# A second level of the seven-product scheme in one product of a down projection

## The chip, the cores and the metric

The kernel runs on 1 core of a Trainium2 chip. The metric is the device time in microseconds (us) of one execution; three runs of the kernel before gave 717.07, 717.15 and 718.08 us, a median of 717.15. Engines are named as in the profile: PE is TensorE (matmuls), PEld its weight loads, DVE VectorE, ACT ScalarE, POOL GpSimd, SP SyncE (here only a DMA queue).

## The reference

One transformer-like block over x of 2048 rows by 1024 columns, in bf16:

```python
xn = _layernorm(x, axis=-1)
s = _A_ref(xn, A_wqkv, A_wo)      # attention: 32 heads of 32; each row sees 8 rows, 2 apart, back; softmax; @ wo
g = _silu(_B_ref(xn, B_w1, B_w3, B_w2))
return x + s * g
def _B_ref(x, w1, w3, w2):        # w1, w3: 1024 x 3584; w2: 3584 x 1024
    gate = jnp.einsum("bsd,df->bsf", x, w1)
    up = jnp.einsum("bsd,df->bsf", x, w3)
    h = _silu(gate) * up
    return jnp.einsum("bsf,fd->bsd", h, w2)
```

The change is in the last line of `_B_ref`, the down projection `h @ w2`.

## The kernel before, in words

**Work.** The 2048 rows are worked through as two blocks of 1024 rows (`b` = 0, 1); a block is two chunks of 512 rows ("row" 0 and 1; chunks are counted c = 0 to 3), and a chunk is four groups of 128 rows (`g`). Every block goes through the q, k, v projections, the up projections, the down projection (`mlp_down`) and, chunk by chunk, attention and the output projection `wo`. The attention itself (products, logits, softmax, weighted sums) is DVE work that fills the time beside PE's matmuls of other stages: chunk 0's beside block 0's up projection, chunk 1's beside block 0's down projection and block 1's q, k, v, and so on.

**Seven products instead of eight.** Every large product is already done by the scheme of Strassen and Winograd at one level: operands are cut in halves (rows, inner dimension, columns), DVE forms sums S1 to S4 of the left operand and T1 to T4 of the right one, and seven half-size products replace eight. In `mlp_down` the left operand is h, 1024 rows by 3584 (28 tiles of 128, FH = 14 in a half), the right one w2, 3584 by 1024 (two column halves of CH = 512). S1 to S4 are formed by DVE in the stage itself (lines 1018 to 1023 and 1033); T1 to T4 were formed while block 0's q projection ran and lie in DRAM (`t_dram`). The seven products follow one another on PE, each as 4 groups x 14 matmuls of 512 columns: h00 w00 into banks `pa` (line 1016), h01 w10 (1026), S2 T2 into `pb` (1035), **S1 T1 into `pe` (1040 to 1044)**, then into `pe` again the product with w2's second half (1055, its right operand called V here), S3 T3 and T4's product into `pb` (1060, 1066). ACT and DVE copy and add the banks between (`dsu`, `dsp`, `dsb`, `dsa`).

**S1** lies in `xs` and part of `xT` (block 0: one place per group; block 1: in `xT`, two groups side by side; `s1v`, line 976).

**Buffers.** The right operands are loaded by SP into a ring of six buffers of 8 KB per partition (pool `r8`): every load takes the two next free buffers, 7 tiles (NQ) each. In block 0 the same ring also holds the rows of chunks 2 and 3 (`xn[0]`, `xn[1]`, called x2 and x3 here), which are normalised in the stage and turned into `xT` by transposing DMAs issued by ACT (`ln_turn`, line 520; `turn2_0` to `turn2_3` after the products marked ("pr", 4 + g), chunk 3's after ("pr", 12) and ("pr", 15)).

**What sets the order.** The program lists its operations with what they read and write (`plan.op`, `tt` for a DVE sum, `cp` for an ACT copy, `dma`). `Plan.place` gives each slot of a pool the buffer that was last used longest ago, and everything that uses the new slot waits for everything that used the old one. PE keeps the order of the listing. For the other engines and queues `Plan.limits` works out when each operation is due (back from PE's order), and `Plan.simulate` runs a clock: whenever an engine is free it takes, of the operations that are ready by that clock, the one that is due first. That order is then written into the program and the chip keeps it: an engine does its instructions in the planned order, whatever is ready. `plan.soon` makes named operations due earlier, `plan.rank` puts named ones first, `plan.chains` puts one after another. In that clock all DMAs go through one pipe:

```python
            if o.nbytes:
                pipe = max(pipe, T + occ + 0.9) + o.nbytes / o.rate
                o.done = pipe + 1.3
```

with `o.rate` 3e5 bytes per us in this stage, and `hop` adds 0.1.

Of the kernel before, what the change touches and what calls it, by code (L numbers as in the profile page):

```python
# [209 lines left out]
def kernel(  # L210
# [737 lines left out]
    def mlp_down(b):  # L948
        G = range(NST)
        R = [range(0, FH), range(FH, FT)]  # L950
        F_ = [slice(0, FH), slice(FH, FT)]
        gs = [[slice(rr * CH + g * P, rr * CH + (g + 1) * P) for g in G] for rr in range(2)]

        def rhs_load(kind, fh=0, dh=0, t=0):
            res = []
            for q in range(FH // NQ):
                wt = plan.slot("r8", f"d{kind}")
                dt = FP16 if kind == "t" else BF16
                v = lambda wt=wt, dt=dt: r8v(wt, dt)[:, 0:NQ * CH].rearrange("p (k n) -> p k n", k=NQ)
                if kind == "t":  # L960
                    dma(SP, "t2", v, lambda q=q: t_dram[:, q * NQ:(q + 1) * NQ, t, :],
                        [("td", i) for i in range(q * NQ, (q + 1) * NQ)], [wt], 896)
                else:
                    f = fh * FH + q * NQ
                    dma(SP, "w2", v, lambda f=f: w2_r[:, f:f + NQ, dh * CH:(dh + 1) * CH], [], [wt], 896)
                res.append((wt, [lambda k=k, v=v: v()[:, k, :] for k in range(NQ)]))
            return res

        def prod(ps, g, row, fh, rhs, first, dt, mark=()):
            src = h_sb if dt == BF16 else h16  # L970
            for q, (wt, ops) in enumerate(rhs):
                fs = range(fh * FH + q * NQ, fh * FH + (q + 1) * NQ)
                mm(ps, [lambda f=f: src[:, f, gs[row][g]] for f in fs], ops, first and q == 0,
                   [wt] + h_cells(fs, row, [g]), last=q == 1, mark=mark)

        def s1v(g):

            if b + 1 == NB:
                return xT16[:, g // 2].rearrange("p k n -> p (k n)")[:, 0:FH * 256].rearrange(
                    "p (f n) -> p f n", f=FH)[:, :, (g % 2) * P:(g % 2 + 1) * P]  # L980
            if g < 3:
                return xs[:, g].rearrange("p k n -> p (k n)")[:, 0:FH * P].rearrange("p (f n) -> p f n", f=FH)
            return xT16[:, 1, 0:FH // 2, CH // 2:CH].rearrange("p k (s n) -> p k s n", s=2)

        def s1_k(g, k):
            return s1v(g)[:, k // 2, k % 2, :] if b + 1 < NB and g == 3 else s1v(g)[:, k, :]

        def s1_cells(g):
            if b + 1 == NB:
                return [("xT", g // 2, f, g % 2) for f in range(FH)]  # L990
            return xs_cells(g) if g < 3 else xt_cells(1, 0, 2) + xt_cells(1, 1, 2) + xt_cells(1, 0, 3) + xt_cells(1, 1, 3)

        def fit(g, a):

            return (lambda: a().rearrange("p (k s) n -> p k s n", s=2)) if b + 1 < NB and g == 3 else a

        hb = lambda fh, row, g: (lambda: h_sb[:, F_[fh], gs[row][g]])
        hf = lambda fh, row, g: (lambda: h16[:, F_[fh], gs[row][g]])
        hcl = lambda fh, row, g: h_cells(R[fh], row, [g])
        NS = FH * P  # L1000
        rhs = rhs_load("w", 0, 0)
        xn = []
        for c in range(2 * b + 2, 2 * b + 4 if b + 1 < NB else 0):
            xt = plan.slot("r8", f"x{c}")
            xn.append(xt)
            for st in range(NST):
                x_load(c, st, xt)
            plan.shift = -5.0
            ln_act(c, range(NST), xt)
            plan.shift = 0.0  # L1010
        pa, pb = [], []
        for g in G:
            if g == 2:
                flush()
            pa.append(bank(f"da{b}_{g}"))
            prod(pa[g], g, 0, 0, rhs, True, BF16)
        for g in G:
            tt("s1", add, lambda g=g: s1v(g), fit(g, hb(0, 1, g)), fit(g, hb(1, 1, g)), hcl(0, 1, g) + hcl(1, 1, g), s1_cells(g), NS, True)
            tt("s3", sub, hf(0, 1, g), hb(0, 0, g), hb(0, 1, g), hcl(0, 0, g) + hcl(0, 1, g), hcl(0, 1, g), NS, True)
        for g in G:  # L1020
            pb.append(bank(f"db{b}_{g}"))
            cp("dfork", pb[g].ap, pa[g].ap, [pa[g]], [pb[g]])
            tt("s2", sub, fit(g, hf(0, 0, g)), lambda g=g: s1v(g), fit(g, hb(0, 0, g)), s1_cells(g) + hcl(0, 0, g), hcl(0, 0, g), NS, True)
        rhs = rhs_load("w", 1, 0)
        for g in G:
            prod(pa[g], g, 0, 1, rhs, False, BF16, [("pr", 4 + g)])
            if b + 1 < NB:
                ln_turn(2 * b + 2, g, xn[0], ("pr", 4 + g))
            gsilu(2 * b, 0, g, pa[g].ap, [pa[g]], 0.48)
        rhs = rhs_load("t", t=T2)  # L1030
        su2 = []
        for g in G:
            tt("s4", sub, hf(1, 0, g), hb(1, 0, g), hf(0, 0, g), hcl(1, 0, g) + hcl(0, 0, g), hcl(1, 0, g), NS, True)
        for g in G:
            prod(pb[g], g, 0, 0, rhs, False, FP16, [("pr", 8 + g)])
            su2.append(plan.slot("k2", "dsu"))
            cp("dsu", lambda g=g: f32(su2[g]), pb[g].ap, [pb[g]], [su2[g]])
        rhs = rhs_load("t", t=T1)
        pe, sp5 = [], []
        for g in G:  # L1040
            pe.append(bank(f"de{b}_{g}"))
            for q, (wt, ops) in enumerate(rhs):
                mm(pe[g], [lambda g=g, k=k: s1_k(g, k) for k in range(q * NQ, (q + 1) * NQ)], ops, q == 0,
                   [wt] + s1_cells(g), last=q == 1, mark=[("pr", 12 + g)])
            if b + 1 < NB and g == 0:
                ln_turn(2 * b + 3, 0, xn[1], ("pr", 12))
                ln_turn(2 * b + 3, 1, xn[1], ("pr", 12))
            if b + 1 < NB and g == 3:
                ln_turn(2 * b + 3, 2, xn[1], ("pr", 15))
                ln_turn(2 * b + 3, 3, xn[1], ("pr", 15))  # L1050
            sp5.append(plan.slot("k2", "dsp"))
            cp("dsp", lambda g=g: f32(sp5[g]), pe[g].ap, [pe[g]], [sp5[g]])
        rhs = rhs_load("w", 1, 1)
        for g in G:
            prod(pe[g], g, 0, 1, rhs, False, FP16, [("pr", 16 + g)])
            tt("dsb", add, lambda g=g: f32(su2[g]), pe[g].ap, lambda g=g: f32(su2[g]), [pe[g], su2[g]], [su2[g]], 512, False)
            gsilu(2 * b, 1, g, lambda g=g: f32(su2[g]), [su2[g]], 0.54)
        rhs = rhs_load("t", t=T3)
        for g in G:
            prod(pb[g], g, 1, 0, rhs, False, FP16, [("pr", 20 + g)])  # L1060
            tt("dsa", add, lambda g=g: f32(sp5[g]), pb[g].ap, lambda g=g: f32(sp5[g]), [pb[g], sp5[g]], [sp5[g]], 512, False)
            gsilu(2 * b + 1, 1, g, lambda g=g: f32(sp5[g]), [sp5[g]], 0.54)
        rhs = rhs_load("t", t=T4)

        def t4(g):
            prod(pb[g], g, 1, 1, rhs, False, BF16, [("pr", 24 + g)])
            gsilu(2 * b + 1, 0, g, pb[g].ap, [pb[g]], 0.48)

        def t4_last():

            g = NST - 1
            dst, wr = gate(2 * b + 1, 0, g)
            prod(pb[g], g, 1, 1, rhs, False, BF16)
            for h in range(2):
                silu("dgh", half(dst, h), half(pb[g].ap, h), [pb[g]], wr + [("gate", h)], 0.25)

        last = b + 1 == NB
        for g in G[:-1] if last else G:
            t4(g)
        return t4_last if last else None  # L1080
# [4 lines left out]
    def wo_tc(q):  # L1085
        return h_cells([2 * q, 2 * q + 1], 0) + h_cells([2 * q, 2 * q + 1], 1)

    def wo_load():

        wots = []  # L1090
        for dh in range(2):
            wot = plan.slot("r8", f"wo{dh}")
            dma(SP, "wo", lambda wot=wot: wot.ap().rearrange("p (j n) -> p j n", j=NJ),
                lambda dh=dh: wo_r[:, :, dh * CH:(dh + 1) * CH], [], [wot], 1024)
            wots.append(wot)
        return wots
# [178 lines left out]
    for nm in "qk":  # L1275
        for j in range(4):
            plan.rank[f"fsnap{nm}{j}"] = len(plan.rank)
    plan.chains.append("qs5q0 qs5q1 qforkq0 qforkq1".split())
    for st in range(NST):
        if st == 2:  # L1280
            ln_mix(0, 2, x0)
# [18 lines left out]
    for b in range(NB):  # L1300
# [43 lines left out]

        def first(b=b):
            if b:
                w1o.extend(wo_load())
            else:
                up_load(b, 0)

# [6 lines left out]
            up_step(b, fb)  # L1357
        attention(c0)
        t4_last = mlp_down(b)
        wots = wo_load()  # L1360
        wo_sums(wots)
        wo(c0, wots)
    attention(3)
    wo(3, wots, last=t4_last)
    flush()
    plan.soon = {n + c: -200.0 for c in "03" for n in ("L", "z", "tr", "zd", "exp", "rec", "pb", "E")}
    plan.run()


# [28 lines left out]
```

## Time and profile before

| | us |
|---|---|
| runs: lowest, median, highest | 717.07, 717.15, 718.08 |
| the profiled execution: span from first to last instruction | 715.3 |
| PE busy, DVE busy, ACT busy in that span | 707.4, 643.8, 382.3 |
| block 0's down projection, PE, from and to | 250.6 to 337.0 |
| its S1 T1 product | 288.6 to 300.7 |
| block 1's S1 T1 product | 639.1 to 651.2 |
| the last matmul starts | 711.6 |

The profile holds one execution's span; its time with what lies around it isn't recorded, so the span is set beside the median, 1.85 us above it. Times in the views are counted from the span's start. A timeline row has the start, the length, the engine, the source line, the operation with what it writes and reads (`out<-in`, by the names of pools and tensors: `r` is the r8 ring, `mm` the PSUM banks, `k` the k2 pool, `a` the attention pool), the form and the count; in brackets, how long the engine had been idle before it and what ended that. The line is mostly that of a helper (L322 the matmul of `mm`, L331 the sum of `tt`, L336 the copy of `cp`, L359 `dma`, L523 `ln_turn`), so operations are told apart by tile, form and time. Engines overlap successive instructions a little, so a row's start is a better measure than its length.

### The profile page before, as it was taken

How to read it: one execution, taken by the hardware profiler on the slowest of the kernel's cores; microseconds unless marked ns; L12 is line 12 of the kernel's file. 1: busy time of each engine (PE TensorE's matmuls, PEld its weight loads, DVE VectorE, ACT ScalarE, POOL GpSimd, SP SyncE). 2: the span in 40 equal slices, each digit the busy share in tenths (PEclk: the TensorE clock that was granted, in tenths of full speed). 3: DMA queues.
4: the chain of work that ended last, by engine and by line, in shares of the span. 5: the costliest groups of instructions: out<-in, count | busy, mean ns of one | idle time of the engine just before them, and what ended most of it. 6: DMA issues, size and time to landing. Idle time of an engine off the chain costs nothing.

```text
span 715.3 us, 9199 instructions
## 1 busy us (share of the span) xinstructions
PE 707.4 (99%) x3287; PEld 343.0 (48%) x3342; DVE 643.8 (90%) x866; ACT 382.3 (53%) x650; POOL 50.7 (7%) x103
## 2 busy tenths in 40 slices
PE   9999999999999999999999999999999999999998
PEld 5555544444444444444555554444444444444443
DVE  7999999997999999599999999676999995899936
ACT  7644556575656799142545354676565654411133
POOL 1020100202000000202000000211000002200000
PEclk9999999999999999999999999999999999999999
DMA  9999966659644758994553569787537347655502
GB/s 331 290 358 345 350 224 203 222 155 300 207 148 169 258 181 237 212 269 125 174 170 131 180 198 337 261 283 244 173 129 239 114 153 213 214 191 177 177 21 97
DMA packets 132205, 151.34 MB, mean 212 GB/s; under 512 B 17216, under 2 KB 109248, under 8 KB 127808
## 3 DMA queue, kind: packets, MB, share of 16 engines
q1 hardware_dynamic: 117168, 121.98, 53.4%
q0 software_dynamic: 6112, 26.22, 10.2%
q10 hardware_dynamic: 8880, 2.56, 1.8%
q8 instruction: 26, 0.43, 0.2%
q14 instruction: 19, 0.16, 0.1%
HBM read 106.96 MB, written 32.51 MB: 195 GB/s over the span
## 4 chain that ended last, share of the span: by engine, by line
PE 99%; issue 0%; DVE 0%; ACT 0%; DVEq 0%
PE mm L322 97%; PE mm L307 1%; PE mm L501 0%; DVE xT L331 0%; ACT xT L508 0%; DVE r L435 0%; PE mm L347 0%; DVE k L305 0%; ACT small L424 0%; DVEq L1393 0%; DVE small L426 0%; DVE eps_t L290 0%; DVE eps_d L291 0%; DVEq L331 0%
## 5 line engine op out<-in xcount | busy, mean ns | idle before, releaser
L322 PEld LDWEIGHTS <-r 128*128 128x128 f16 (+1 forms) x2276 | 240.0, 107 | 244.5 <-DMA r<-in_A_wqkv_dram 0.5
L322 PE MATMUL mm<-xs,r 128*128 128x512 f16 x1280 | 295.2, 379 | 0.0
L322 PE MATMUL mm<-xT,r 128*128 128x512 bf16 (+2 forms) x956 | 224.3, 371 | 2.1
L336 ACT COPY k<-mm 128x512 f32<-128x512 f32 x192 | 112.4, 586 | 93.5 <-PE mm L322 93.0
L322 PE MATMUL mm<-r,h_sb 128*128 128x512 bf16 (+1 forms) x694 | 153.0, 379 | 0.5
L322 PEld LDWEIGHTS <-h_sb 128*128 128x128 f16 (+1 forms) x800 | 78.3, 98 | 94.4
L336 ACT COPY mm<-mm 128x512 f32<-128x512 f32 (+1 forms) x89 | 50.6, 571 | 72.2 <-PE mm L322 68.2
L331 DVE TENSOR_TENSOR a<-a,a 128x2048 bf16<-128x2048 bf16 (+1 forms) x72 | 87.7, 1218 | 0.3
L331 DVE TENSOR_TENSOR a<-qo,kT 128x2048 bf16<-128x2048 bf16 x64 | 77.4, 1219 | 1.4 <-ACT kT L336 1.3
L331 DVE TENSOR_TENSOR a<-E,vT 128x2048 bf16<-128x2048 bf16 x56 | 66.4, 1217 | 0.0
L331 DVE TENSOR_TENSOR k<-mm,k 128x512 f32<-128x512 f32 x72 | 48.1, 684 | 19.9 <-PE mm L322 19.8
L331 DVE TENSOR_TENSOR h_sb<-mm,k 128x512 bf16<-128x512 f32 x96 | 63.0, 684 | 1.0 <-PE mm L322 0.5
L353 ACT ACTIVATE k<-k 128x512 bf16<-128x512 f32 x56 | 34.9, 631 | 45.6 <-DVE k L331 45.6
L331 DVE TENSOR_TENSOR h_sb<-h_sb,k 128x1024 bf16<-128x1024 bf16 x56 | 37.1, 686 | 17.2 <-ACT k L336 17.2
L331 DVE TENSOR_TENSOR r<-r,r 128x1024 f16<-128x1024 f16 (+5 forms) x61 | 49.5, 818 | 0.9 <-DMA xT<-r 0.5
L353 ACT ACTIVATE h_sb<-mm 128x512 bf16<-128x512 f32 x60 | 35.8, 598 | 21.7 <-PE mm L322 21.6
L331 DVE TENSOR_TENSOR a<-a 128x1024 bf16<-128x1024 bf16 (+4 forms) x60 | 37.9, 633 | 6.8 <-ACT a L754 4.4
L336 ACT CAST k<-mm 128x512 bf16<-128x512 f32 x56 | 32.6, 585 | 12.2 <-PE mm L322 12.1
L331 DVE TENSOR_TENSOR qo<-qo,a 128x2048 bf16<-128x2048 bf16 x32 | 38.9, 1216 | 0.0
L359 POOL DMA_DIRECT2D a<-E x32 | 16.7, 528 | 303.6 <-ACT k L336 126.1
L331 DVE TENSOR_TENSOR h_sb<-h_sb 128x512 f16<-128x512 bf16 (+1 forms) x72 | 37.0, 575 | 0.0
L331 DVE TENSOR_TENSOR r<-r 128x1024 f16<-128x1024 bf16 (+1 forms) x34 | 25.7, 780 | 0.0
(98 smaller groups left out, 387.8 us busy)
## 6 DMA issues: line engine op xcount, KB each, us to landing
r<-in_B_w_dram SPq DMA_DIRECT2D x42, 512.0 KB, 4.3
s_dram<-r POOLq DMA_DIRECT2D x14, 1024.0 KB, 5.4
r<-t_dram SPq DMA_DIRECT2D x16, 896.0 KB, 6.1
r<-s_dram SPq DMA_DIRECT2D x14, 1024.0 KB, 4.8
r<-in_B_w_dram SPq DMA_DIRECT2D x12, 896.0 KB, 4.9
r<-in_A_wqkv_dram SPq DMA_DIRECT2D x10, 1024.0 KB, 7.3
h_sb<-in_B_w_dram SPq DMA_DIRECT2D x14, 512.0 KB, 8.9
t_dram<-h_sb POOLq DMA_DIRECT2D x14, 512.0 KB, 6.5
```

The lines of the kernel that those rows point to most:

```text
L307: nc.tensor.matmul(plan.pools["mm"][i % 8][:], lhsT=warm[:, 0:P], rhs=warm[:, 0:CH], start=True, stop=True)
L322: nc.tensor.matmul(cut(ps.ap()), lhsT=lhs[k](), rhs=cut(rhs[k]()), start=(first and k == 0), stop=(last and k == n - 1), skip_group_check= ...
L331: plan.op(DVE, name, lambda: fn(out=o(), in0=a(), in1=b()), rd, wr, occ, 0.08, late=late)
L336: plan.op(ACT, name, lambda: nc.scalar.copy(out=o(), in_=a()), rd, wr, occ, 0.11)
L353: plan.op(ACT, name, lambda: nc.scalar.activation(out=o(), in_=a(), func=ACTF.Silu), rd, wr, occ, 0.11, table="silu")
L359: plan.op(eng, name, lambda: e.dma_start(out=o(), in_=a()), rd, wr, occ, 0.0, nbytes=kb * 1024, late=late)
```

## The change

The product S1 T1 (512 x 1792 by 1792 x 512) is itself done by seven products of half the size, in both blocks. Its operands are cut once more: rows in two pairs of groups (`m`), the 14 inner tiles in even and odd ones (`kk`), the columns in two halves of 256 (`n`). Its T1 load therefore takes every second tile (`fs`), and all of T1 is loaded before. `product2` forms the second level's sums on DVE: u (the sum S1 of this level) and t1 in a new r8 slot `ex`, the others in place. Each of the 14 calls of `p` per block is 7 matmuls of 256 columns (`NQ`). The bank of one group is used in halves of 256 columns, with ACT copies (`l2s15`, `l2fork`, `l2u2`) and DVE adds (`l2c22`, `l2c12`) between. S2 T2's product for the last group, `t2(NST - 1)`, moves between the first four and the last ten of these calls, and the four `dsp` copies and chunk 3's turns stand behind all of them. Apart from that: the loads get names, block 0's first `wo` load is chained behind the second half of T4's load on SP, and chunk 1's logit DMAs and softmax steps get the early due times that chunks 0 and 3 had.

```diff
                 if kind == "t":
-                    dma(SP, "t2", v, lambda q=q: t_dram[:, q * NQ:(q + 1) * NQ, t, :],
-                        [("td", i) for i in range(q * NQ, (q + 1) * NQ)], [wt], 896)
+                    fs = slice(q, FH, 2) if t == T1 else slice(q * NQ, (q + 1) * NQ)
+                    dma(SP, f"t2_{b}{t}{q}", v, lambda fs=fs: t_dram[:, fs, t, :],
+                        [("td", i) for i in range(FH)[fs]], [wt, (wt, 0), (wt, 1)], 896)
...
+        def product2(pe, rhs):
+            ex = plan.slot("r8", "ex")
+            HC = CH // 2
...
+            for a, u, cells, uc, size in rows:
+                tt("l2s1", add, u, a(1, 0), a(1, 1), cells(1, 0) + cells(1, 1), uc, size, True)
+            in_place((1, 0), (0, 0), True, "l2s3")
+            tt("l2t1", sub, tv, wv(0, 1), wv(0, 0), [(w[0], 1), (w[0], 0)], [(ex, 0)], NQ * HC, True)
+            tt("l2t3", sub, wv(0, 1), wv(1, 1), wv(0, 1), [(w[1], 1), (w[0], 1)], [(w[0], 1)], NQ * HC, True)
...
+            def p(ps, n, A, B, first=False, mark=()):
...
+                    for k in range(NQ):
+                        nc.tensor.matmul(half(ps.ap, n)(), lhsT=a[k](), rhs=c[k](), start=first and k == 0, stop=k == NQ - 1,
+                                         skip_group_check=True)
...
+            for i in I:
+                p(pe[2 + i], 0, lhs(0, 0, i), rw(0, 0), True)
+            for i in I:
+                p(pe[2 + i], 1, lhu(i), rt)
+            in_place((0, 0), None, True, "l2s2")
+            tt("l2t2", sub, wv(0, 0), wv(1, 1), tv, [(w[1], 1), (ex, 0), (w[0], 0)], [(w[0], 0)], NQ * HC, True)
...
+                cp("l2s15", lambda i=i: f32(s15[i]), pe[2 + i].ap, [pe[2 + i]], [s15[i]])
+                cp("l2fork", half(pe[i].ap, 0), lambda i=i: f32(s15[i])[:, 0:HC], [s15[i]], [pe[i]], 0.33)
+            yield
+            for i in I:
+                p(pe[i], 0, lhs(0, 1, i), rw(1, 0))
+                p(pe[2 + i], 0, lhs(0, 0, i), rw(0, 0), mark=[("pr", 12)] * i)
+                cp("l2u2", half(pe[i].ap, 1), half(pe[2 + i].ap, 0), [pe[2 + i]], [pe[i]], 0.27)
+            in_place((0, 1), (0, 0), False, "l2s4")
+            tt("l2t4", sub, wv(1, 0), wv(1, 0), wv(0, 0), [(w[1], 0), (w[0], 0)], [(w[1], 0)], NQ * HC, True)
+            for i in I:
+                p(pe[2 + i], 0, lhs(1, 0, i), rw(0, 1))
+                tt("l2c22", add, half(pe[2 + i].ap, 1), half(pe[2 + i].ap, 0), lambda i=i: f32(s15[i])[:, HC:CH],
+                   [pe[2 + i], s15[i]], [pe[2 + i]], HC, False)
+            for i in I:
+                p(pe[i], 1, lhs(0, 1, i), rw(1, 1))
+                tt("l2c12", add, half(pe[i].ap, 1), half(pe[i].ap, 1), lambda i=i: f32(s15[i])[:, HC:CH],
+                   [pe[i], s15[i]], [pe[i]], HC, False)
+            for i in I:
+                p(pe[2 + i], 0, lhs(1, 1, i), rw(1, 0), mark=[("pr", 15)] * i)
...
-        for g in G:
+        def t2(g):
             prod(pb[g], g, 0, 0, rhs, False, FP16, [("pr", 8 + g)])
...
-        rhs = rhs_load("t", t=T1)
+        for g in G[:-1]:
+            t2(g)
+        rhs1 = rhs_load("t", t=T1)
         pe, sp5 = [], []
         for g in G:
             pe.append(bank(f"de{b}_{g}"))
-            for q, (wt, ops) in enumerate(rhs):
-                mm(pe[g], [lambda g=g, k=k: s1_k(g, k) for k in range(q * NQ, (q + 1) * NQ)], ops, q == 0,
-                   [wt] + s1_cells(g), last=q == 1, mark=[("pr", 12 + g)])
...
+        steps = product2(pe, rhs1)
+        next(steps)
+        t2(NST - 1)
+        for _ in steps:
+            pass
+        if b + 1 < NB:
+            for g in G:
+                ln_turn(2 * b + 3, g, xn[1], ("pr", 12 if g < 2 else 15))
+        for g in G:
             sp5.append(plan.slot("k2", "dsp"))
             cp("dsp", lambda g=g: f32(sp5[g]), pe[g].ap, [pe[g]], [sp5[g]])
...
+    plan.chains.append("t2_021 wo0_0".split())
...
-    plan.soon = {n + c: -200.0 for c in "03" for n in ("L", "z", "tr", "zd", "exp", "rec", "pb", "E")}
+    plan.soon = {n + c: -200.0 for c in "013" for n in ("L", "z", "tr", "zd", "exp", "rec", "pb", "E")}
```

`in_place(x, y, neg, name)` subtracts the two named quarters of S1 into the first (in block 0 one DVE instruction of 896 elements for each group of the pair, in block 1 one of 1792 for both; the same holds for `l2s1`); with `y` None the other operand is u.

## The prediction

> **What bounds the kernel now.** I read the page's parts 1, 2 and 4 first, then the chain of waits in order of time, then the timelines of the engines around the first block's S1 x T1 product (288.6 to 300.7 us) and around the end.
>
> ```profile
> PE 707.4 (99%) x3287; PEld 343.0 (48%) x3342; DVE 643.8 (90%) x866; ACT 382.3 (53%) x650; POOL 50.7 (7%) x103
> ...
> PEclk9999999999999999999999999999999999999999
> ...
> PE 99%; issue 0%; DVE 0%; ACT 0%; DVEq 0%
> ```
>
> TensorE (PE) is busy for 99% of the span and carries 99% of the chain that ended last, at full clock in all 40 slices. So the time is the sum of the matmuls: a matmul taken out is gained in full, and a wait that PE gets is paid in full. DVE is the second engine, at 90%.
>
> What a matmul costs is read from two stretches of PE's timeline, the S1 x T1 product of block 0 and the last eight matmuls:
>
> ```profile
> 288.61 9.23 PE L322 MATMUL mm<-r,xs 128*128 128x512 f16 x42
> ```
>
> ```profile
> 710.80 1.04 PE L347 MATMUL mm<-h_sb,qo 128*128 128x256 f16 x8
> ```
>
> The columns are start, length, engine, line, form, count. A matmul of 512 columns lasts 379 ns, but the next starts before it ends: (9.23 - 0.379)/41 = 0.2159 us from one to the next. For 256 columns (272 ns each, a weight load of 98 ns before each): (1.04 - 0.272)/7 = 0.1097 us. Halving the width halves the step almost exactly.
>
> **The change, part by part.**
>
> *Matmuls.* Both blocks together lose 2 x 56 of 512 columns (112 x 0.2159 = 24.18 us) and get 2 x 14 x 7 = 196 of 256 columns (196 x 0.1097 = 21.50 us). Gain 2.68 us, 1.34 in each block, all on the path if PE doesn't wait.
>
> *New DVE work.* The rows that price it (count, busy us, mean ns):
>
> ```profile
> L331 DVE TENSOR_TENSOR h_sb<-h_sb 128x1792 f16<-128x1792 bf16 x16 | 16.7, 1083 | 0.0
> ...
> L331 DVE TENSOR_TENSOR r<-r,r 128x1024 f16<-128x1024 f16 x14 | 9.6, 687 | 0.0
> ...
> L331 DVE TENSOR_TENSOR xT<-mm,xs 128x256 bf16<-128x256 f32 x2 | 0.8, 424 | 0.9 <-PE mm L347 0.9
> ```
>
> DVE overlaps successive instructions by 0.08 us (in its timeline the next starts that much before the end), so a 1792-element sum takes 1.00 us of it. For 896 elements there is no row: between the 512-element form (418 ns) and the 1024-element one (687) a straight line gives 0.62, or 0.54 of DVE. Block 0 gets 4 of 1792 (the l2t), 8 of 896 (the l2s) and 4 adds of 256 columns from PSUM (0.34): 4.0 + 4.3 + 1.4 = 9.7 us; block 1 gets 8 of 1792 and 4 adds, 9.4 us. ACT gets, per block, 2 copies of 512 (586 ns) and 4 of 256 columns (the one 256-column row has 357): 2.6 us, where its timeline shows 2.4 us free after each copy.
>
> Two holes of DVE take its 9.4 to 9.7 us:
>
> ```profile
> 287.69 0.68 DVE L331 TENSOR_TENSOR a<-a 128x1024 bf16<-128x1024 bf16 x1
> ...
> 303.99 0.69 DVE L331 TENSOR_TENSOR k<-mm,k 128x512 f32<-128x512 f32 x1 [8.74 <-PE mm L322]
> ```
>
> ```profile
> 690.77 0.69 DVE L331 TENSOR_TENSOR r<-mm,k 128x512 bf16<-128x512 f32 x1 [9.88 <-ACT k L336]
> ```
>
> In block 0 DVE stands idle 8.74 us while chunk 1's logits are turned by DMA; the chunk's last products move into it, and its softmax starts some 9 us later. That is what the new `soon` entry answers: its 16 + 16 small DMAs (8 of each 16 on SP, 5.0 us a set) and its DVE steps now go first. Chunk 1's last sum ended at 399.2 and its output product starts at 420, so 20 us cover it; uncovered, each us late would cost one. In block 1 the 9.4 us push the softmax-weighted sums of chunk 3 behind chunk 2's output sums, into the 9.88 us hole before 690.77; chunk 3's product needs them at 693. Without that hole the end would come several us later. Cost of DVE's load on the path: 0.
>
> *Loads.* T1's two halves are issued at 275.21 and 276.72 as before and have landed by 284.1; the first half product now starts at 285.6. V (w2's second load) passes through the buffer that `ex` now holds first: issued near 293 instead of 281.48, 4.9 us to landing by the page's part 6 (6.6 for a second one behind it), needed at 301.7. `wo` waits for T4's second half on SP: 2 to 3 us later than 311.47, for sums that PE needs at 340. All hidden.
>
> *The wait that is added.* The first two half products (S1 and T1 as they are) start when `t2(2)` ends: 276.52 + 42 x 0.2159 = 285.59, and end 14 x 0.1097 later, at 287.12. The next needs u and t1 in `ex`. At that point of the program five of the six r8 buffers are held, so `ex` is the one that held x2 until its last transposing DMA (`turn2_3`). On the chip that DMA lands early: SP's next load of this buffer left at 281.48.
>
> ```profile
> 275.21 1.87 SPq L359 DMA_DIRECT2D r<-t_dram  x2
> 281.48 6.18 SPq L359 DMA_DIRECT2D r<-in_B_w_dram  x2
> ```
>
> But DVE runs in the order that `Plan.simulate` writes, and that puts all DMAs through one pipe at 0.3 MB/us: from 276.0 (three turns issued just before the 275.46 silu, and 0.9), four turns of 0.87 and two halves of T1 of 3.06 end at 285.6, landing 1.3 later, 286.9. Before that no sum into `ex` can be picked. At 286.4 DVE takes another chunk-1 product (1.14 us), and only at the place of the row at 287.69 above comes t1 (due first, being longer), then u of g = 2. So on the chip: t1 at 287.69, u at 288.69, u's end 289.31, the weight load some 0.1 us and the hand-over 0.05 (near 8.6 us a DVE result released PE that quickly) after it: **PE waits from 287.12 to 289.45, 2.3 us**. Everything of PE is queued behind. Ends: 0 if DVE came first (rival A), 3.5 if one more 1.2 us DVE instruction slips in.
>
> In block 1 the buffer comes free at 625.7 (V's load is issued then) and S1 is done by 625.0, 12 us ahead of need: no wait.
>
> *The hand-overs after it.* In block 1 S4 can start when PE's second S1-half product ends (644.65), takes 1.08, and is needed at 646.7: 0.9 us in hand, against 1.22 us instructions that DVE doesn't interrupt. T4 behind it has 0.5 in hand, the first dsp 1.1. In block 0 S4 is in two parts and has over 2 us, but ACT's first dsp now stands behind two transposes of chunk 3, moved from 291.89 to about 297.3 by their mark:
>
> ```profile
> 291.89 3.52 ACTq L523 DMA_TRANSPOSE xT<-r  x2
> ```
>
> They hold ACT's queue 3.5 us, to 300.8; dsp ends at 301.4 and PE wants it at 301.7 (it starts V's product 1.0 us later than before). I put 0.15 us in each block: half of what a mean slip of 0.6 leaves open. Bounds 0 and 2.1 in all (rival B).
>
> **Sum**, against the profiled span of 715.3 us: -2.68 + 2.3 + 0.3 = -0.1 us. The three runs before have a median of 717.15, 1.85 over that span; I take these 1.85 as unchanged and forecast **717.0 us**. The forecast's own range is 716.0 to 718.0.
>
> **Rivals.**
> A: *the wait in block 0 is not there*, because DVE forms t1 and u before 286 (the buffer is free at 281.5 on the chip, and a planned order that knew it would do so). Then -2.68 + 0.3: 714.8 us. Against it is the planner's formula above; for it, that DVE has 7 us of deferrable chunk-1 work there.
> B, the slower side: *the second-level sums come late behind DVE's long instructions*. Place: S4, T4 and c12/dsp in block 1, dsp in block 0. It decides where a sum starts over 0.9 us after its release. If each slips the full 1.22: S4 0.3, T4 0.7, dsp 0.1, and 1.0 in block 0, 2.1 in all instead of 0.3: 718.8 us, and 719.2 with a wait of 2.7. For it: DVE has no idle stretch between 612 and 671. Against: the due times put these sums ahead of all attention work.
> C, slower too: *PE's clock drops in the wait*. The first twelve matmuls (12 in 5.30 us, 0.44 each) ran at half rate for 5.3 us; such a stretch costs 2.6: 719.6 us. No row here has an idle PE of 2.3 us in mid-run; gaps of 0.4 to 0.8 near 7 to 9 us did not slow what followed. The Trainium skill, "TensorE: Matmul & The Clock Gate", section "What's actually happening", puts the drop after an idle window of about 3.4 us; by that rule a 2.3 us wait leaves the clock alone, and C dies. No run shown can test it yet.
> That the change does less than it says (a half product left out or not narrower) is excluded by its counts: 14 products of 7.
>
> **How the numbers follow.** Forecast 0.57, A 0.20, B 0.15, C 0.05, others 0.03. 0.2% of 717.15 is 1.4 us, about what a measurement of this kernel can tell from no change: faster means below 715.7. Faster: A and a little of the forecast (a wait of under 1 us), 0.22. Same: 0.57. Slower: B, C and the rest, 0.21. Range: A to B, 714.6 to 719.1.
>
> **What would show it.** Right: 98 matmuls of 256 columns per block at 0.11 us; in block 0 one PE gap of about 2.3 us near 287.1, ended by DVE `r<-` or its weight load, with a 1792-element DVE sum starting at 287.7; in block 1 no gap over 0.3; PEclk all 9. DVE's holes at 295 and 681 shrink. Wrong: no gap near 287 (A); gaps near 646 to 650 ended by DVE or ACT (B); matmuls of 0.22 us per 256 columns after the gap (C); an idle PE at 690 to 700 would mean that the DVE load doesn't fit.

## The result, and the profile after

The changed kernel takes **721.6 us** (median of four runs; 721.36 to 721.8) beside 717.53 of the kernel before: a ratio of 1.0057 [1.0044, 1.0070], slower by 4.1 us, where 717.0 was forecast (714.6 to 719.1). The profiled execution's span went from 715.3 to 719.9. The ratios of the experiments are against the kernel before as it ran beside them (medians 717.42 to 717.66).

The lines of the page after that answer to those of before (engines, granted clock, chain that ended last):

```profile
PE 707.3 (98%) x3426; PEld 350.5 (49%) x3426; DVE 660.3 (92%) x894; ACT 386.8 (54%) x662; POOL 50.6 (7%) x103
...
PEclk9999999999999999999999999999999999999999
...
PE 82%; DVE 8%; DMA 7%; issue 1%; ACTq 1%; SPq 0%; ACT 0%; DVEq 0%
```

PE's busy share fell by only one point, but the chain is no longer PE alone: 15% of it now runs through DVE and DMAs. In order of time, the DMA pieces are loads at the start (2.62 to 21.21) and, later, transfers at whose end PE goes on (305.71 to 320.05 and 321.35 to 329.46; 344.15 to 352.44, with a sum of DVE behind it). The DVE pieces are nearly all at the end of the kernel, from 654 on. PE's view of waits, after:

```profile
PE mm L322 <- ACT k L336: 2.5, 1, 2.5
PE mm L322 <- DVE r L331: 1.6, 2, 1.4
PE mm L322 <- DMA r<-t_dram: 1.4, 1, 1.4
PE mm L307 <- DVE k L305: 1.3, 1, 1.3
...
```

The columns are who waited for whom, the sum in us, how often, the longest; three smaller rows (the start, the tail) are left out. Only the last of the four (PE's start) is in the kernel before. The other three are in and just behind block 0's down projection (of the 1.6 us, 1.40 are there and 0.21 in the tail). PE's timeline there, after (the wait before a row stands in brackets):

```profile
285.88 1.69 PE L1054 MATMUL mm<-r,xs 128*128 128x256 f16 x14
287.41 1.69 PE L1054 MATMUL mm<-r 128*128 128x256 f16 x14
288.94 3.19 PE L322 MATMUL mm<-r,h_sb 128*128 128x512 f16 x14
...
298.84 0.93 PE L1054 MATMUL mm<-r,xT 128*128 128x256 f16 x7
302.25 2.10 PE L322 MATMUL mm<-r,h_sb 128*128 128x512 bf16 x9 [2.48 <-ACT k L336]
```

```profile
329.50 10.73 PE L322 MATMUL mm<-r,h_sb 128*128 128x512 f16 x49 [1.41 <-DMA r<-t_dram]
...
353.74 1.92 PE L322 MATMUL mm<-xs,r 128*128 128x512 f16 x8 [1.40 <-DVE r L331]
```

The row at 287.41 is the product with t1 and u, which was to wait 2.3 us: it follows without a gap. DVE forms t1 and the first part of u just ahead of it:

```profile
285.63 1.10 DVE L331 TENSOR_TENSOR r<-r 128x1792 f16<-128x1792 f16 x1
286.64 0.64 DVE L331 TENSOR_TENSOR r<-xs 128x896 f16<-128x896 f16 x1
```

A product of seven matmuls takes 0.765 us (two in the 1.53 us from 285.88 to 287.41), 0.109 each, as priced. The half-width products end at 299.77, and there PE stops 2.48 us for V's product, which needs ACT's first copy dsp. T4's second half (329.5) and the first sum on wqkv (353.7) are the next stops. A wait is counted from the end of the matmul before it, which lies 0.16 us behind the point at which the next could have started (0.379 less 0.216); with these the three make 5.8 us.

A ledger shows where time goes: how much later than before PE starts the same matmul, read from the timelines at four marks (before: 24.43 near the start; 376.69 and 684.47, behind block 0 and behind block 1's products; 710.80, the last eight matmuls).

| kernel, median us | start | behind block 0 | behind block 1's products | last eight |
|---|---|---|---|---|
| changed, 721.6 | +0.30 | +4.70 | +3.31 | +4.07 |
| e1, 716.49 | -0.04 | -0.78 | -2.17 | -1.41 |
| e2, 718.86 | -0.05 | +1.72 | +0.33 | +1.10 |
| e3, 715.65 | -0.15 | -0.15 | -1.53 | -1.53 |
| e4, 723.34 | +0.46 | +3.72 | +3.72 | +4.71 |
| e5, 716.27 | +0.09 | -0.65 | -2.03 | -1.28 |
| e6, 721.40 | +0.48 | +4.30 | +2.92 | +3.67 |
| e7, 717.91 | -0.25 | +0.83 | -0.55 | -0.55 |
| e8, 714.40 | -0.02 | -1.41 | -2.80 | -2.80 |
| e9, 719.76 | +0.47 | +4.41 | +3.03 | +3.02 |
| e10, 715.62 | -0.12 | -1.51 | -2.88 | -2.12 |

Row "changed": block 0 loses 4.40 (5.79 of waits against a gain of 1.39), block 1 gains 1.39 in full, the tail loses 0.76. The start's differences (-0.25 to +0.48) come ahead of all that was changed.

Why is dsp late? Before, chunk 3's four transposing DMAs held ACT's queue 3.52 us from 291.89 and 5.02 us from 300.96. ACT's timeline after:

```profile
295.23 6.34 ACTq L523 DMA_TRANSPOSE xT<-r  x2
301.61 0.58 ACT L336 COPY k<-mm 128x512 f32<-128x512 f32 x1 [6.04 <-DVE a L331]
301.76 3.91 ACTq L523 DMA_TRANSPOSE xT<-r  x1
302.09 1.57 ACT L336 COPY k<-mm 128x512 f32<-128x512 f32 x3
305.71 4.47 ACTq L523 DMA_TRANSPOSE xT<-r  x1
```

"ACTq" rows are ACT's queue busy with issuing. Chunk 3's first two transposing DMAs hold it for 6.34 us, to 301.57 (the first 1.47, the second 4.84), and dsp (the copy at 301.61) stands right behind; the releaser in the brackets is only the last semaphore event that the profile saw. The planner counts 0.1 us of ACT's time for such a DMA (the 0.1 in `ln_turn`'s `plan.op`), so in its clock the two cost dsp nothing. What runs beside them is seen on SP's queue after:

```profile
290.64 1.75 SPq L359 DMA_DIRECT2D r<-in_B_w_dram  x2
292.45 7.71 SPq L359 DMA_DIRECT2D r<-t_dram  x3
307.24 13.29 SPq L359 DMA_DIRECT2D a<-E  x8
320.63 0.62 SPq L359 DMA_DIRECT2D r<-in_A_wo_dram  x1
321.35 0.60 SPq L359 DMA_DIRECT2D r<-t_dram  x1
```

V's two loads left at 281.48 and 287.29 before; now `ex` has x2's buffer, so the first takes that of T2's first half (which PE reads until about 290.5, since S2 T2's last group has moved behind the first half-width products) and the second takes `ex`'s own. They leave from 290.64 on, with T3 and half of T4 behind them: five large loads leave between 290.64 and 300.16, and chunk 3's first two transposes at 295.23 and 296.73. The theory T is that this crowd stretches the transposes; their hold of ACT makes the first wait; their late landing (x3's buffer and rows come free at 320) makes the second, since T4's second half takes x3's buffer and leaves at 321.35, and the third, since chunk 3's sums and chunk 1's softmax follow late on DVE and SP. Rivals: R1, the order of the half-width products itself; R2, the tail, where DVE's 16.5 us of added busy time are the bound; R3, the order on ACT's queue alone.

### The profile page after: what moved, and what is told of

Read it like the earlier page. It is cut to its first block, busy times and chain, and to the rows that moved or that the text cites. A ratio compares the mean times of both kernels' runs of the same rounds, so it can differ in the third digit from the quotient of the medians.

```text
span 719.9 us, 9455 instructions
## 1 busy us (share of the span) xinstructions
PE 707.3 (98%) x3426; PEld 350.5 (49%) x3426; DVE 660.3 (92%) x894; ACT 386.8 (54%) x662; POOL 50.6 (7%) x103
## 4 chain that ended last, share of the span: by engine, by line
PE 82%; DVE 8%; DMA 7%; issue 1%; ACTq 1%; SPq 0%; ACT 0%; DVEq 0%
PE mm L322 80%; DMA r<-in_A_wqkv_dram 4%; DVE a L331 3%; PE mm L1054 2%; DMA xT<-r 2%; DVE qo L331 1%; DMA r<-t_dram 1%; DVE h_sb L331 1%; DVE r L331 1%; DVE xT L331 1%; ACTq L523 1%; DVE k L331 1%; SPq L359 0%; ACT k L336 0%; DVEq L331 0%
## 5 line engine op out<-in xcount | busy, mean ns | idle before, releaser
L322 PE MATMUL mm<-xT,r 128*128 128x512 bf16 (+1 forms) x996 | 227.1, 372 | 0.9 <-DMA r<-in_A_wqkv_dram 0.9
L336 ACT COPY k<-mm 128x512 f32<-128x512 f32 x196 | 114.3, 586 | 87.6 <-PE mm L322 75.2
L331 DVE TENSOR_TENSOR a<-qo,kT 128x2048 bf16<-128x2048 bf16 x64 | 79.0, 1246 | 0.0
L331 DVE TENSOR_TENSOR r<-r,r 128x1024 f16<-128x1024 bf16 (+5 forms) x67 | 56.7, 856 | 2.1 <-DMA r<-in_A_wqkv_dram 1.2
L331 DVE TENSOR_TENSOR r<-r 128x1024 f16<-128x1024 bf16 (+2 forms) x36 | 28.2, 813 | 0.0
```

The source lines that it names most:

```text
L322: nc.tensor.matmul(cut(ps.ap()), lhsT=lhs[k](), rhs=cut(rhs[k]()), start=(first and k == 0), stop=(last and k == n - 1), skip_group_check= ...
L331: plan.op(DVE, name, lambda: fn(out=o(), in0=a(), in1=b()), rd, wr, occ, 0.08, late=late)
L336: plan.op(ACT, name, lambda: nc.scalar.copy(out=o(), in_=a()), rd, wr, occ, 0.11)
```

## The experiments

**e1: without chunk 3's transposes.**

```
-        plan.op(ACT, f"turn{c}_{st}", lambda: nc.scalar.dma_start(
+        plan.op(ACT, f"turn{c}_{st}", lambda: None if c == 3 else nc.scalar.dma_start(
```

> The changed kernel without the four transposing DMAs of block 1's second chunk (chunk 3), so that chunk works on stale rows; all else, the written order too, is as in the changed kernel. Theory T (block 0's three new gaps on PE, 2.64 us at 302, 1.57 at 329.5 and 1.56 at 353.7, all descend from those four transposes, which hold ACT's queue from 295.2 to 310.2 and land at 305 to 320): none of the three gaps is left, the time is 721.6 less some 5.5 us, about 716.1 (715.3 to 717). Rival R1 (the gap at 302 comes from the order of the products in the changed block and from dsp itself, the other two from DMA traffic that stays): at most one of the gaps goes, the time stays above 719. Rival R2 (the loss is the tail, where VectorE is the bound from 654 on): the three gaps go, but the tail keeps its finish; the time stays above 719.

Measured: 716.49 us, ratio 0.9989 [0.9979, 0.9998]. The gaps at 302 and 329 are gone; a wait of 0.46 at 348 is what is left of the third. All three descend from the four transposes, the third but for 0.46; R1 falls, and R2 explains at most the tail's 0.76, which is still there (-2.17 to -1.41).

**e2: dsp ahead of the transposes on ACT.**

```
-            cp("dsp", lambda g=g: ...
+            cp(f"dsp{b}_{g}", lambda g=g: ...
+    plan.chains.append("dsp0_0 dsp0_1 dsp0_2 dsp0_3 turn3_0 turn3_1 turn3_2 turn3_3".split())
```

> The changed kernel with ACT's four copies dsp of block 0 put ahead of the four transposing DMAs of chunk 3 in ACT's order; nothing else is touched. Theory T: PE's gap at 302 (2.64 us) goes to below 0.5, but the transposes start about 6 us later, so that x3 lands later and the gaps at 329.5 and 353.7 (1.57 and 1.56) stay or grow: 719 to 723, nearest 720.5. Rival R3 (only the order on ACT's queue is wrong, and the later gaps follow from the hold of the queue, not from the traffic): all three gaps go, 715.5 to 717.

Measured: 718.86, 1.0027 [1.0016, 1.0037], just under the foreseen range. V's product follows without a gap:

```profile
298.79 0.93 PE L1054 MATMUL mm<-r,xT 128*128 128x256 f16 x7
299.56 6.64 PE L322 MATMUL mm<-r,h_sb 128*128 128x512 bf16 x29
```

The two later waits stay (1.37 and 1.14 us). So the first wait is ACT's queue and costs 2.6 (block 0 loses 1.77 instead of 4.40); R3 falls for the rest.

**e3 and e4: the products in one block alone.** The other block gets back its 512-column products (even and odd column tiles as the two halves of T1):

```
-        steps = product2(pe, rhs1)
+        if b == 1:      (e4: b == 0)
+            steps = product2(pe, rhs1)
...
+            t2(NST - 1)
+            for g in G:
+                for q, (wt, ops) in enumerate(rhs1):
+                    mm(pe[g], [lambda g=g, k=k: s1_k(g, k) for k in range(q, FH, 2)], ops, q == 0, ...)
```

> Seven half-size products in block 1 alone, where no second chunk is transposed next to them; block 0 computes S1 T1 as before the change. Theory T: none of the gaps at 302, 329 and 354, the gain of one block (56 x 0.2159 - 98 x 0.1097 = 1.34 us) is kept but for some 0.3 us at the tail: 716.2 to 716.8 beside 717.5 before. Rival R2 (tail, bound by VectorE): the same or slower than before, 717.5 to 719.5.

> Seven half-size products in block 0 alone; block 1 computes S1 T1 as before the change. Theory T: the three gaps (5.8 us) are there, the gain is that of one block (1.34 us): 721.5 to 723, nearest 722. Rival R2 (tail): near 716.5.

Measured: e3 715.65, 0.9978 [0.9968, 0.9987], better than foreseen: block 1 gains its whole 1.38 and its tail loses nothing. e4 723.34, 1.0092 [1.0067, 1.0118], worse than foreseen, though its waits in block 0 (2.04 and 0.57) are smaller than the changed kernel's; its four executions spread from 721.82 to 725.85, and the profile is of one of 722.35. In that one some 1.7 us more are lost to PE's clock behind the first wait. Stretches of e4 (us, then busy time with counts by engine, granted clock, DMA share, GB/s):

```profile
298.00:300.00 2.00, 1.93 (x18) 1.55 (x17) 2.00 (x5) 0.00 (x0) 0.00 (x0) 1.00 1.07 349
300.00:302.00 2.00, 0.03 (x1) 0.05 (x2) 2.00 (x4) 0.67 (x2) 0.00 (x0) 1.00 1.22 241
302.00:304.00 2.00, 1.95 (x6) 0.78 (x7) 2.00 (x3) 1.39 (x3) 0.00 (x0) 0.71 1.17 251
304.00:306.00 2.00, 2.00 (x6) 0.76 (x5) 0.20 (x1) 0.00 (x0) 0.00 (x0) 0.50 1.12 271
...
308.00:310.00 2.00, 2.00 (x11) 0.93 (x10) 0.70 (x3) 0.00 (x0) 1.08 (x3) 1.00 1.33 110
```

PE stands still from 300 to 302, and then does 6 matmuls in 2 us instead of 11, at a granted clock of 0.5 (from about 302.9 to 306.3, by stretches of 0.5 us).

**e5: without V's loads.** `dma` emits nothing for block 0's two loads of V.

```
+        dma(SP, "V0" if b == 0 and (fh, dh) == (1, 1) else "w2", v, ...)      (an operation named V0 emits nothing)
```

> The changed kernel without block 0's two loads of V (w2's second column half of the second sum), so block 0's V product works on what is left in those buffers; order and all else as in the changed kernel. Theory T1 (ACT's hold by the transposing DMAs, 1.5 + 4.8 us for the first two, is stretched by the loads that run beside them; V's two, late because ex has x2's buffer, are the ones that were not there before the change): without V the first two transposes leave ACT's queue by about 299 as before the change (2.2 us and less each), dsp starts before 300, the gap at 302 shrinks from 2.5 to under 0.8, and the later ones with it: 716.5 to 719. Rival T2 (the hold comes from T3's loads, which stand beside the transposes in any case, or from the transposes themselves): the second transpose still holds ACT over 4 us, the gap stays over 2 us: 720.5 to 722.

Measured: 716.27, 0.9986 [0.9977, 0.9995]. ACT's queue:

```profile
295.02 2.77 ACTq L523 DMA_TRANSPOSE xT<-r  x2
298.26 1.56 ACT L336 COPY k<-mm 128x512 f32<-128x512 f32 x3 [2.89 <-DVE mm L331]
```

The same two transposes, issued at the same time, hold it 2.77 us instead of 6.34, dsp starts at 298.26, and the three waits are gone but for 0.46 at 348. T3's two loads leave at about the same times (291.95 and 296.54; in the changed kernel 292.45 and 296.74). T1 holds: the crowd made by V's late loads is what stretches the hold. What is stretched is the first transpose's way to landing (3.2 us here, 10.0 in the changed kernel) and with it the second's hold (1.48 us here, 4.84 there). T2 falls.

**e6: the ranking undone.**

```
-    plan.soon = {n + c: -200.0 for c in "013" ...
+    plan.soon = {n + c: -200.0 for c in "03" ...
```

> The changed kernel with the second part of the change undone: chunk 1's softmax ranked as before, the seven products in both blocks. If the ranking costs (its 16 small DMAs of the probabilities, E1, go ahead of wqkv's second half on SP and so make the gap at 353.7, 1.4 us): 720 to 720.5, the gap at 353.7 gone. If the ranking changes nothing, since by the planner's own order these DMAs fall in the same place: 721.2 to 722, gap and all. The second is the likelier: the planned order on SP differs only behind E1's third DMA.

Measured: 721.40, 1.0061 [1.0046, 1.0077]: in sum the ranking changes nothing. Its own share stays open. In this execution the wait at 302 was 2.85, the clock was at 0.5 for about 3.4 us, as in e4, and the wait at 353 was only 0.46; PE came later to it.

**e7: the first two transposes earlier.**

```
-                ln_turn(2 * b + 3, g, xn[1], ("pr", 12 if g < 2 else 15))
+                ln_turn(2 * b + 3, g, xn[1], ("pr", (10 if b == 0 else 12) if g < 2 else 15))
```

> The changed kernel with the first two of chunk 3's four transposing DMAs marked behind the third T2 product (as early as 286, a stretch in which no load runs) instead of behind the product that follows the fork; the other two stay. Theory T: issued beside no load they leave ACT's queue in 1.3 to 2 us each and land by 292, dsp is not held, the gap at 302 is gone (below 0.5), and x3 lands some 3 to 6 us earlier; the gap at 329.5 shrinks below 0.8; at 348 to 354 the planner's own stall of 1.9 us stays: 717.5 to 719. Rival R1 (the gap at 302 comes from the products' own order): the gap stays over 2, 721 or more.

Measured: 717.91, 1.0009 [0.9999, 1.0018]; its executions fall into two groups: five of 716.57 (the profiled one) to 717.21 with a mean granted clock of 0.999 or 1.000, and five of 718.62 to 719.68 with one of 0.997. The first two transposes leave at 282.58 and 283.93 and hold the queue 1.25 and 2.88 us; the waits at 302 and 329 are gone. The third wait has grown to 2.28, at 349.9: the planner, with chunk 1's probability DMAs ahead of wqkv's second half, plans DVE to form another sum first (a stall of 1.9 us in its own order).

**e8: four orders mended.** e7's edit, and

```
-    plan.chains.append("t2_021 wo0_0".split())
+    plan.rank["wqkv0_1z"] = 7
+    plan.chains.append("wqkv0_1z E1s01 E1s03 E1s11 E1s13 E1s21 E1s23 E1s31 E1s33".split())
+    plan.chains.append("t2_021 wo0_1 wo0_0".split())
...
-    plan.soon = {n + c: -200.0 for c in "013" ...
+    plan.soon = {n + c: -200.0 for c in "0123" ...
```

(the names with z and s are given to wqkv's second half in block 1 and to SP's eight probability DMAs of chunk 1.)

> The changed kernel with four orders mended, its work the same: chunk 3's first two transposes as in e7, T4's second half ahead of both halves of wo on SP, wqkv's second half ahead of chunk 1's eight probability DMAs on SP, and chunk 2's softmax ranked soon too (the tail). Theory T (the seven products gain 2.7 us in both blocks and all that was lost is order on three queues): no gap over 0.5 us from 256 to the end, 714.5 to 716, nearest 715.0, faster than before. Rival R2 (VectorE's added 19 us set the end): 717 or more, with gaps behind 690.

Measured: **714.40 us**, 0.9960 [0.9947, 0.9972], faster than both kernels and just under the foreseen range. Its page and its view of waits:

```profile
PE 704.6 (99%) x3371; PEld 351.0 (49%) x3426; DVE 659.6 (93%) x894; ACT 386.5 (54%) x662; POOL 50.8 (7%) x103
...
PE 98%; DVE 1%; issue 0%; DMA 0%; DVEq 0%
```

```profile
PE mm L307 <- DVE k L305: 1.3, 1, 1.3
PE mm L501 <- DVE r L435: 0.2, 1, 0.2
```

Only the waits at PE's start are left, as before the change, and by the ledger each block gains 1.39 and the tail loses nothing. DVE is at 93% and yet costs nothing: R2 falls.

**e9: the predicted wait, made true.** e8 and chunk 2's transposes due as late as before the change:

```
-            [(xt, st), cell], xt_cells(half, 0, st) + xt_cells(half, 1, st), 0.1, 0.0, nbytes=256 * 1024)
+            [(xt, st), cell], xt_cells(half, 0, st) + xt_cells(half, 1, st), 0.1, 0.0, nbytes=256 * 1024, late=8.5 if c == 2 else 0.0)
```

> The mended kernel (e8) with one more edit: chunk 2's four transposing DMAs get back the due time that they had before the change (8.5 us later), so that the planner's order lets them pass behind DMAs and copies as before, and DVE's list of work forms t1 and u behind one more product of chunk 1. This makes the condition of the predicted wait true. The prediction's step: PE waits near 287 for 2.3 us and everything slips: e8's 714.4 + 2.2 = 716.6 (716.2 to 717.2; some executions 1.5 to 2 us more if the granted clock falls behind the wait as it did behind the 2.0 and 2.85 us waits of e4 and e6). Rival: on the chip the transposes land early whatever their due time, DVE takes t1 and u in time, and the time stays at 714.4 to 715.

Measured: 719.76, 1.0032 [1.0021, 1.0042], 5.4 more than e8 and above the foreseen range. PE's and DVE's timelines:

```profile
286.05 1.69 PE L1055 MATMUL mm<-r,xs 128*128 128x256 f16 x14
291.23 2.21 PE L1055 MATMUL mm<-r 128*128 128x256 f16 x14 [3.48 <-DVE r L331]
293.23 3.11 PE L322 MATMUL mm<-r,h_sb 128*128 128x512 f16 x8
```

```profile
286.14 1.22 DVE L331 TENSOR_TENSOR a<-a,a 128x2048 bf16<-128x2048 bf16 x1
287.28 2.35 DVE L331 TENSOR_TENSOR a<-qo,kT 128x2048 bf16<-128x2048 bf16 x2
289.55 1.08 DVE L331 TENSOR_TENSOR r<-r 128x1792 f16<-128x1792 f16 x1
290.55 0.62 DVE L331 TENSOR_TENSOR r<-xs 128x896 f16<-128x896 f16 x1
```

The wait is at the predicted place, and t1 (the row at 289.55) stands behind chunk-1 products, two more of them than in e8's order. But the order isn't all: the last of chunk 2's transposes now leaves at 278.61 and lands 10.9 us later, at 289.5 (in e8 it leaves at 275.55 and has landed by 283.7), so t1, which goes into that buffer, couldn't have come sooner in any order. The run shows that the due time makes the wait, not that DVE's order alone does. It is 3.48 instead of 2.3 (the prediction had 3.5 with one more product ahead), and the granted clock is at 0.50 to 0.66 from 292 to 296 behind it, which makes up the rest (5.3 us between e8's and e9's marks).

**e10: e8 without its fourth edit** (`"013"` again).

> The mended kernel (e8) without its fourth edit: chunk 2's softmax ranked as in the changed kernel. If the tail's loss of the changed kernel (0.76 us between 688 and the end, with gaps of 0.2 at 697 and 702) came from chunk 2's and chunk 3's attention being late behind the added sums, it is back: 714.9 to 715.3, and the small gaps behind 690 are there. Rival: the tail's loss followed from block 0's delay, and this one runs like e8: 714.3 to 714.6.

Measured: 715.62, 0.9971 [0.9960, 0.9982], just above the foreseen range. Of the 1.2 us more than e8 the ledger shows 0.76 as the tail's loss, which is back (-2.88 to -2.12) with its small waits:

```profile
691.46 2.75 PE L322 MATMUL mm<-r,qo 128*128 128x512 bf16 x11 [0.21 <-DVE r L331]
...
696.13 5.38 PE L322 MATMUL mm<-h_sb 128*128 128x512 f16 x24 [0.18 <-DVE h_sb L331]
```

The rest, 0.5, lies behind the last eight matmuls: from their start to the end of the span it is 5.1 us here and 4.5 in e8. So the loss isn't a consequence of block 0's delay, and in e8's order the rank of chunk 2's softmax decides it. It doesn't in every order: e3 (with the added sums in block 1) and e7 have the changed kernel's rank and lose nothing in the tail, and e4, which has no added sums in block 1, loses 0.99.

## Why the prediction was wrong

- **Matmuls (gain 2.68): right.** 1.39 and 1.39 in the ledger, 2.78 in e8.
- **New DVE work, cost 0: nearly right.** The 896-element sum, put at 0.62, measures 0.64; the 1792-element one 1.10. The work fits in block 0. At the end it was put at 0, and PE lost 0.76 there, with another 0.5 behind the last matmuls. The rank of chunk 2's softmax takes this away (e8 against e10), but e3, e4 and e7 show that neither the rank nor the sums of block 1 are the whole cause.
- **The wait that is added (2.3): the step that failed first.** Its working took the due times of the kernel before. But `ex` has x2's buffer, so t1 and u wait for chunk 2's transposes, and the due time of these moves 8.5 us earlier with theirs; the planner sends three of them out sooner (on the chip at 265.32, 267.74 and 271.86; before at 270.47, 271.84 and 273.23), and DVE has t1 at 285.63 and the first part of u at 287.28, which PE takes at 287.41. e9 gives the transposes back the old due time, and the wait is there. Rival A was right that it isn't, but by 0.1 us: t1 and u were not formed before 286.
- **Loads, all hidden: wrong.** V's loads land in time for PE (the wait at 302 is for ACT). That the first leaves 9 us later, close to chunk 3's transposes, was worked out (near 293), but only PE's need was asked, not what they would run beside. So T4's second half, which takes x3's buffer, left at 321.35 instead of 313.74, and PE waited 1.41 us for it; the sums on wqkv came late by 1.40. By the ledger the two cost 3.15 us where 0 was put.
- **The hand-overs: the mis-sized term.** "They hold ACT's queue 3.5 us, to 300.8" took the hold from a stretch with fewer loads: it is 6.34, to 301.57, and 2.77 without V (e5). The wait that didn't come has no part in this: the transposes leave behind ACT's copy of one of PE's products, so both they and PE's coming to V's product were earlier than forecast (295.23 for 297.3, 299.77 for 301.7), and after a hold of 3.5 us dsp would have ended at about 299.4, before PE came. For the 0.15 us put here the first wait cost 2.64. Block 0 lost 5.79 instead of 2.3 + 0.15, so rival A's 714.8 fell with the forecast: it took the first wait away and asked for nothing behind it. Rival B had the right place (dsp, 1.0 us) but neither its cause nor the two waits further on.
- **Rival C, the clock.** It didn't decide here: the changed kernel's profile shows 1.00 in every stretch, behind a wait of 2.48 too, and its other executions, with mean clocks of 0.998 to 0.999, took no longer. But it is real: with waits of 2.04 (e4), 2.85 (e6) and 3.48 us (e9) came a clock of 0.5 for about 3.4 us, which cost 1.6 to 1.7 us each, and e7's two groups of executions, some 2 us apart, differ in their clock.

By the prediction's terms: -2.78 + 0 (for 2.3) + 2.64 (for block 0's 0.15) + 3.15 (for the loads' 0) + 0 (for block 1's 0.15) + 0.76 (for 0, the tail) + 0.30 at the start = +4.07, which is what the last mark shows; 0.5 behind it makes up the span's 4.6.

The Trainium skill, "TensorE: Matmul & The Clock Gate", section "What's actually happening", puts the fall to half clock after an idle window of about 3.4 us, and says that the window is free-running. The prediction used it to rule rival C out for a wait of 2.3 us. e9's 3.48 us agrees with it; e4 and e6 don't (half clock with stops of 2.04 and 2.85 us), and by the changed kernel's 2.48 without a fall such a shorter wait doesn't always do it. The measurement decides: a wait of 2 us may cost nearly twice its length.

That loads on SP stretch transposes that ACT issues fits what the Trainium skill says in "DMA: Bandwidth & Descriptors", section "Rules for kernel authors": DMAs of different issuing engines run on the same 16 DMA engines and interleave. The trace agrees (6.34 against 2.77 us with and without V's loads). That the issuing engine's own queue is held meanwhile is shown by the ACTq rows here.

Open: the ranking's own share (e6; e3 has it too and loses nothing), what makes the tail's loss beside the rank, and why the 8 small DMAs of chunk 1's logits took SP 13.29 us to issue where they took 4.99 before. Three of them left within 0.03 us of a transpose's landing, and some did so in e2, e8 and e9, as if they waited for it; this was not tried.

## What to carry to other kernels

Where a program writes the order from due times, a new reader or a new holder of a buffer moves the due times of all that comes before it: work these through again before a wait is read from the old order. Ask of every transfer that a change delays not only who needs it but what it now runs beside, above all DMAs whose issue holds an engine's queue. Take such a hold from a stretch with as many transfers beside it. A product that costs 2.8 us less is worth nothing until the queues around it are in order again (721.6 against 714.4 with the same work).

## What the runs showed of the hardware

- Of two transposing DMAs of 256 KB issued one right behind the other, the second held ACT's queue longer, if not strictly in proportion, where the first landed later: 1.48 us where the first landed after 3.2 us (e5), 2.88 after 5.4 (e7) and 4.84 after 10.0 (the changed kernel, with four loads of 896 KB on their way during that hold); 3.65 after 10.5 (e9's last pair). The first of each of these pairs held it 1.25 to 1.47 us; e8's third transpose held it 1.25 us with three such loads on their way. ACT's copies behind them wait as long.
- With a stop of PE of 2.04 to 3.48 us the granted clock went to 0.5 for about 3.4 us in three profiles (e4, e6, e9; in e4 and e9 it fell 0.9 and 1.0 us after PE had started again) and stayed at 1.00 in two others (the changed kernel with 2.48, e7 with 2.28).
